# Larger first transfers, a new order of loads and weights, and exponentials kept in PSUM, in a fused gated-attention and feed-forward kernel

## The chip, the cores and the metric

The kernel runs on one core of a Trainium2 chip. The core has five engines that run side by side and meet only at semaphores: TensorE (PE, matrix products; PEld is its loading of weights), VectorE (DVE), ScalarE (ACT), GpSimd (POOL) and SyncE (SP, which here issues transfers). Transfers between main memory and the on-chip memory SBUF are carried by 16 DMA engines. PE writes its results to PSUM, a second on-chip memory of eight banks[...].

The metric is the device time of one execution in microseconds (us), as a median over runs. All line numbers are those of the kernel before.

## What is computed

Two stages, one behind the other. The first is a recurrence over time with a forget gate per channel; the second is a feed-forward layer on its result, with a gate through a ReLU.

```python
# q, k, v, f_logit: 4 batches x 8 heads x 768 steps x 48 channels
f = 1.0 / (1.0 + np.exp(-f_logit))
state = zeros((B, H, D, D))
for t in range(S):
    state = f[:, :, t, :, None] * state + einsum('bhd,bhe->bhde', k[:, :, t], v[:, :, t])
    y[:, :, t] = einsum('bhd,bhde->bhe', q[:, :, t], state)

x = y.transpose(0, 2, 1, 3).reshape(3072, 384)
gate = maximum(x @ w_gate, 0.0)          # 384 x 1536
val = x @ w_val                          # 384 x 1536
out = gate * val @ w_out                 # 1536 x 384
```

Inputs and output are float32; the products run in bfloat16.

## The kernel before

**Steps.** Time is cut into six steps of 128 (`c` from 0 to 5). A step covers 128 positions of all four batches, 512 tokens. Inside a step the recurrence becomes matrix products. With `bneg = ln(1 + exp(-f_logit))`, the negative logarithm of the gate, PE forms running sums over the 128 positions (`cum`), ACT takes `exp(-sum)` for q and `exp(+sum)` for k, and the products of q and k with these go into the tile `hats`. The hats are transposed into `qkT`; PE forms scores from them, DVE masks the scores into `ptm`, PE forms `y` from `ptm`, from `vpad` (a padded bfloat16 copy of v, made by POOL) and from the state of the step before. ACT copies `y` to `xT`, the input of the feed-forward part. There PE multiplies with `wg` (gate), ACT takes the ReLU, PE multiplies with `wv` (value), DVE multiplies both into `gT` (all near L784 to L807), PE multiplies with `wo` (L819), ACT copies the result out of PSUM (L829) and SP stores it (L833).

**Step 0 is built in another way than the rest** (`fours = (0,)`, `attention_four`, L485). Its f, k and q come in with four successive positions of one head in one piece of 768 bytes, so that partition 4t+b holds positions 4t to 4t+3 of batch b. The loader `load_four` (L375) issues four transfers per tensor, one per batch. The step is worked in two halves of the heads, `hh`, and in each half in two pairs of positions, `z`. For each (hh, z) ACT makes the exponentials for q (L532, written to `expo` in SBUF) and those for k (L535, in place in PSUM); the product with q is done by POOL for z=0 and by DVE for z=1 (L538), the one with k by DVE (L543). L555 transposes, L564 (DVE) and L563 (ACT) copy to `qkT`, L574 forms scores, L581 masks, L733 forms `y`, L750 makes `xT`.

**Loads of later steps** (`load`, L393) bring one tensor for two batches each ("f1.0" is f of step 1, batches 0 and 1), in pieces of 192 bytes, issued by SP. **Weights** come in nine blocks (`wg0` to `wo2`), issued by POOL (`load_w`, L409), converted to bfloat16 on the way. The order of the first transfers is written by hand:

```python
first = ("f0 k0 q0 v0.0 v0.1 wg0~8.0 wv0~8.5 wg1~14.5 wv1~15.3 wg2~17.5 wv2~18.3 f1.0@wv1 k1.0 q1.0 v1.0 "
         "wo0~23 wo1~25.5 f1.1@wo0 k1.1 wo2~28 q1.1 v1.1").split()
```

A number after `~` is the earliest time at which the planner may place the issue; `@wv1` makes SP wait until wv1 has landed. Loads from step 2 on wait for the third load before them (`flight = 3`) and for their buffer.

**The order on each engine** comes from a planner (`Plan.schedule`, L90). Every operation is entered with what it reads and writes, a price (`occ`, `lat`), a priority and the PSUM banks that it opens; banks are lent from groups with limits (L294). The planner always takes the operation that can start earliest by its own clock, then the one of lower priority number, and so writes one fixed order per engine. Landing times of transfers are estimates too: a queue in which each transfer takes `flow` us. On the chip each engine follows its order strictly and stops at the semaphore of the first operation that isn't ready. The waits are derived from the plan (`needs`, L171).

**Fillers.** Where the plan leaves PE idle before 17 us, products with a tile of zeros (L880) are put in, so many as fit in the planned gap:

```python
gap, each = op.start - at, 0.44 if at < 4.5 else 0.23
if begun and op.start <= warm_until:
    for _ in range(int((gap - 0.05) / each)):
        busy.append((op, warm))
```

Of the kernel before, what the change touches and what calls it, by code (L numbers as in the profile page):

```python
# [5 lines left out]
AF = mybir.ActivationFunctionType  # L6
# [5 lines left out]
class Op:  # L12
# [1 line left out]

    __slots__ = ("eng", "emit", "reads", "writes", "occ", "lat", "prio", "opens", "deps",
                 "idx", "start", "end", "pos", "inc", "sem", "val", "snap", "n_left", "users", "ready",
                 "after", "follows", "flow", "goal", "floor")

    def __init__(self, eng, emit, reads, writes, occ, lat, prio, opens=(), after=(), follows=()):
        self.eng, self.emit, self.reads, self.writes = eng, emit, reads, writes  # L20
        self.occ, self.lat, self.prio, self.opens = occ, lat, prio, list(opens)
        self.after, self.follows = list(after), list(follows)
        self.users = []
        self.inc = False
        self.sem = None
        self.val = 0
        self.start = None
        self.flow = None
        self.floor = 0.0


class Bank:
# [9 lines left out]
class Plan:  # L42
# [47 lines left out]
    def schedule(self, banks):  # L90
        self.link()
        for op in self.ops:
            op.n_left = len(op.deps)
            op.ready = op.floor
            for d in op.deps:
                d.users.append(op)
        free = dict(self.free0)
        waiting = {e: [] for e in self.ENGINES}
        order = {e: [] for e in self.ENGINES}
        for op in self.ops:  # L100
            if op.n_left == 0:
                waiting[op.eng].append(op)
        slots = [{"ap": ap, "tile": None, "at": at} for ap, at in banks]
        used = {}
        left = len(self.ops)
        flow_free = 0.0

        def banks_for(op):
            n, group = len(op.opens), op.opens[0].group
            if used.get(group, 0) + n > self.limits[group]:  # L110
                return None
            idle = [s for s in slots if s["tile"] is None or all(o.start is not None for o in s["tile"].ops)]
            idle.sort(key=lambda s: s["at"])
            return idle[:n] if len(idle) >= n else None

        while left:
            pick = None
            for e in self.ENGINES:
                for op in waiting[e]:
                    at = max(free[e], op.ready)  # L120
                    slot = ()
                    if op.opens:
                        slot = banks_for(op)
                        if slot is None:
                            continue
                        at = max(at, slot[-1]["at"])
                    key = (at, op.prio, op.idx)
                    if pick is None or key < pick[0]:
                        pick = (key, op, slot)
            if pick is None:  # L130
                raise RuntimeError("no op can be scheduled: " + repr(
                    [(e, len(waiting[e])) for e in self.ENGINES]))
            (at, _, _), op, slot = pick
            e = op.eng
            waiting[e].remove(op)
            for tile, s in zip(op.opens, slot):
                if s["tile"] is not None:
                    for o in s["tile"].ops:
                        op.deps[o] = "war"
                s["tile"] = tile  # L140
                tile.ap, tile.slot = s["ap"], s
                used[tile.group] = used.get(tile.group, 0) + 1
            op.start, op.end = at, at + op.occ + op.lat
            if op.flow is not None:
# [24 lines left out]
        return order  # L169
# [47 lines left out]
def bass_hgrn2_outer__then__ffn_reglu_kernel(  # L217
# [12 lines left out]
    x_way = {0: "tiled", 1: "tiled", 2: "tiled", 3: "xbar", 4: "xbar", 5: "xbar"}  # L230
    flight = 3
    wsteps = 3
    first = ("f0 k0 q0 v0.0 v0.1 wg0~8.0 wv0~8.5 wg1~14.5 wv1~15.3 wg2~17.5 wv2~18.3 f1.0@wv1 k1.0 q1.0 v1.0 "
             "wo0~23 wo1~25.5 f1.1@wo0 k1.1 wo2~28 q1.1 v1.1").split()
    B, H, S, D = q.shape
    C = 128
    NC = S // C
# [53 lines left out]
    zeros = sb("zeros", [128, 512], BF16)  # L291
    banks = [nc.alloc_psum_tensor(f"ps{i}", [128, 512], F32) for i in range(8)]

    pl = Plan({"bc": 2, "bc4": 4, "tp": 2, "tp4": 4, "s": 4, "y": 2, "kv": 1, "f": 4})  # L294
    add = pl.add
    gp, ve, sc, te, sy = nc.gpsimd, nc.vector, nc.scalar, nc.tensor, nc.sync
    engine = {"POOL": gp, "DVE": ve, "ACT": sc}
# [77 lines left out]
    def load_four(n, c):  # L375
        t = ld[n]
        row = NL[n] * 2 * HD

        def go():
            ops = []  # L380
            for b in range(B):
                src = bass.AP(tensor=srcs[n].tensor, offset=b * H * S * D + c * C * D,
                              ap=[[4 * D, 32], [S * D, H], [1, 4 * D]])
                dst = bass.AP(tensor=t, offset=b * row + slot_of(n, c, 0) * 2 * HD, ap=[[4 * row, 32], [4 * D, H], [1, 4 * D]])
                ops.append(sy.dma_start(dst, src))  # L385
            return ops
        last = tails.get("load")
        op = add("SP", go, [], in_keys(n, c, 0, B), occ=1.5, lat=0.9, prio=c * 100, follows=[last] if last else [])
        tails["load"] = op
        dma(op, f"{n}{slot_of(n, c, 0)}", 2.4, 4)  # L390
        return op

    def load(n, c, b0, b1, after=()):  # L393
# [3 lines left out]
                      ap=[[D, C], [S * D, (b1 - b0) * H], [1, D]])  # L397
        dst = t[:, slot_of(n, c, b0 // 2), :, :, :].rearrange("p b h d -> p (b h) d")
        op = add("SP", lambda: sy.dma_start(dst, src), [], in_keys(n, c, b0, b1),
                 occ=0.8 * (b1 - b0), lat=0.9, prio=c * 100, after=after,  # L400
                 follows=[last] if last else [])
        tails["load"] = op
        dma(op, f"{n}{slot_of(n, c, b0 // 2)}", 1.0 * (b1 - b0))
        return op

    WJ = NJ // wsteps
# [2 lines left out]
    def load_w(nm, s, at):  # L409
# [4 lines left out]
        else:  # L414
# [1 line left out]
                          ap=[[DFF, 128], [128 * DFF, NK], [1, WJ * 128]])  # L416
            dst = (wg if nm == "wg" else wv)[:, :, s * WJ * 128:(s + 1) * WJ * 128]
        last = tails.get("load_w")
        op = add("POOL", lambda: gp.dma_start(dst, src), [], [f"{nm}{s}"], occ=0.8, lat=1.2, prio=0,
                 follows=[last] if last else [])  # L420
        op.floor = at
        tails["load_w"] = op
# [3 lines left out]
    loads, done = [], {}  # L426
    for item in first:
        item, _, at = item.partition("~")
        item, _, behind = item.partition("@")
        need = [done[behind]] if behind else []  # L430
        if item[0] == "w":
            op = load_w(item[:2], int(item[2:]), float(at))
        elif "." in item:
            c, pr = (int(x) for x in item[1:].split("."))
            op = load(item[0], c, 2 * pr, 2 * pr + 2, need)
        else:
            op = load_four(item[0], int(item[1:]))
        done[item] = op
        if item[0] != "w":
            loads.append(op)  # L440
# [44 lines left out]
    def attention_four(c):  # L485
# [17 lines left out]
        for hh in range(2):  # L503
# [23 lines left out]
            for z in range(2):  # L527
# [1 line left out]
                ex = expo[:, e0 + i0:e0 + i0 + 2, 0, hh * HD // 2:(hh + 1) * HD // 2]  # L529
                hi = (h0 + i0) % NH  # L530
                his = (hi, hi + 1)
                add("ACT", lambda ex=ex, b_=bc[z]: sc.activation(  # L532
                    ex, b_.ap[:, 0:HD].rearrange("p (i e) -> p i e", i=2), AF.Exp, scale=-1.0), [bc[z]],
                    [f"expq{e0 + i0}_{hh}"], prio=R + z, **act_t(HD))
                add("ACT", lambda b_=bc[z]: sc.activation(b_.ap[:, 0:HD], b_.ap[:, 0:HD], AF.Exp, scale=1.0), [bc[z]],  # L535
                    [bc[z]], prio=R + z, **act_t(HD))
                e = "DVE" if z else "POOL"
                add(e, lambda e=e, ex=ex, hi=hi, hs=hs, i0=i0: engine[e].tensor_tensor(  # L538
                    hats[:, hi:hi + 2, 0, hs, 0:D], by_i["q"][:, i0:i0 + 2, hs, :],
                    ex.rearrange("p i (h d) -> p i h d", h=4), ALU.mult),  # L540
                    key["q"] + [f"expq{e0 + i0}_{hh}"] + [f"hats{x}" for x in his], [f"hq{x}_{hh}" for x in his], prio=R + z + 1,
                    **elem_t(e, HD))
                add("DVE", lambda b_=bc[z], hi=hi, hs=hs, i0=i0: ve.tensor_tensor(  # L543
                    hats[:, hi:hi + 2, 1, hs, 0:D], by_i["k"][:, i0:i0 + 2, hs, :],
# [338 lines left out]
    for op in order["PE"]:  # L883
        gap, each = op.start - at, 0.44 if at < 4.5 else 0.23
        if begun and op.start <= warm_until:
            for _ in range(int((gap - 0.05) / each)):
                busy.append((op, warm))
        begun = True
        at = op.start + op.occ
# [81 lines left out]
```

## Time and profile before

| | |
|---|---|
| median of 13 runs | 209.63 us |
| lowest and highest | 207.66 and 211.77 us |
| the profiled execution | 211.5 us |
| its span, first to last instruction | 209.8 us |
| PE busy | 190.9 us (91%) |
| DVE, ACT, POOL busy | 104.9, 110.4, 79.5 us |
| read from main memory, written to it | 25.95 MB, 4.72 MB |
| mean granted clock of PE | 0.967 of full |

The profile is of one execution. Its time stands 1.9 us above the median, and 1.7 us of it lie around the span. Busy time of PE is not PE at its peak: products with a lower clock, and the 9.1 us of fillers (24 of L880), count as busy.

The issues of transfers, with the median time from issue to landing, are these (KB is the size in SBUF; a weight block is read at twice that):

```profile
v_in<-in_v_dram SPq DMA_DIRECT2D x12, 384.0 KB, 5.3
out_dram<-osb SPq DMA_DIRECT2D x24, 192.0 KB, 2.2
...
wg<-in_moe_w_gate_dram POOLq DMA_DIRECT2D x3, 384.0 KB, 6.6
wv<-in_moe_w_val_dram POOLq DMA_DIRECT2D x3, 384.0 KB, 7.7
wo<-in_moe_w_out_dram POOLq DMA_DIRECT2D x3, 384.0 KB, 12.7
...
f_in<-in_f_logit_dram SPq DMA_DIRECT2D x4, 192.0 KB, 3.0
k_in<-in_k_dram SPq DMA_DIRECT2D x4, 192.0 KB, 3.4
q_in<-in_q_dram SPq DMA_DIRECT2D x4, 192.0 KB, 4.6
```

"SPq" is SP's work of issuing, not the transfer itself. The last three rows are the four pieces each of step 0.

### The profile page before, as it was taken

To read this page: it belongs to the slowest core of one execution; us is meant where nothing else is said; L and a number is where in the kernel's file an instruction comes from. 1 tells how busy PE (TensorE), PEld (TensorE's weight loads), DVE (VectorE), ACT (ScalarE), POOL (GpSimd) and SP (SyncE) were. 2 spreads that over 40 slices of the span, in tenths; PEclk is the share of its full clock that TensorE was granted. 3 is DMA by queue.
4 is the path that set the end of the run, shared out by engine and by line. 5 is a ranking of instruction groups with operands and counts; after the bars stand their busy time and mean duration, and the time that the engine had idled before them with its cause. 6 is when DMAs were issued, how large, how long until landed. Compare 5 with 4: busy or idle time off the path is not lost.

```text
span 209.8 us, 4328 instructions
## 1 busy us (share of the span) xinstructions
PE 190.9 (91%) x1724; PEld 109.7 (52%) x1743; DVE 104.9 (50%) x183; ACT 110.4 (53%) x239; POOL 79.5 (38%) x112
## 2 busy tenths in 40 slices
PE   7824779999999799999999998996999999999994
PEld 2413458645677585455555554553546554445562
DVE  7008377643817969657277353734545333323210
ACT  2840224583488688867738755564434334443411
POOL 8805920026196885966643643323410000000000
PEclk9995858999999999999999999999999999999999
DMA  4999799999589999999899996997962111111112
GB/s 142 260 176 171 106 199 188 193 230 220 138 188 240 197 220 176 183 199 214 177 205 140 194 205 123 219 177 144 194 139 60 54 38 41 38 38 38 38 49 105
DMA packets 115076, 31.74 MB, mean 151 GB/s; under 512 B 105072, under 2 KB 115056, under 8 KB 115056
## 3 DMA queue, kind: packets, MB, share of 16 engines
q1 hardware_dynamic: 111072, 27.93, 65.5%
q0 software_dynamic: 3984, 3.54, 11.0%
q8 instruction: 14, 0.23, 0.5%
q14 instruction: 6, 0.05, 0.2%
HBM read 25.95 MB, written 4.72 MB: 146 GB/s over the span
## 4 chain that ended last, share of the span: by engine, by line
PE 81%; DMA 7%; SPq 4%; ACT 3%; DVE 2%; issue 2%; DVEq 0%
PE ps L796 43%; PE ps L819 21%; DMA q_in<-in_q_dram 4%; SPq L385 3%; PE ps L706 3%; DMA qkT<-hats 3%; PE ps L733 2%; PE ps L767 2%; PE ps L676 2%; PE ps L640 1%; PE ps L555 1%; PE ps L880 1%; PE ps L743 1%; PE ps L739 1%; PE ps L574 1%
## 5 line engine op out<-in xcount | busy, mean ns | idle before, releaser
L806 DVE TENSOR_TENSOR gT<-relu,ps 128x512 bf16<-128x512 bf16 (+1 forms) x82 | 50.5, 620 | 58.5 <-PE ps L796 44.5
L802 ACT ACTIVATE relu<-ps 128x512 bf16<-128x512 f32 (+1 forms) x82 | 44.5, 545 | 31.7 <-PE ps L796 29.2
L796 PE MATMUL ps<-xT,wv 128*128 128x512 bf16 (+1 forms) x243 | 60.2, 355 | 0.3 <-issue 0.2
L796 PE MATMUL ps<-xT,wg 128*128 128x512 bf16 (+1 forms) x231 | 57.6, 355 | 1.4 <-ACT xT L750 0.6
L819 PE MATMUL ps<-wo,gT 128*128 128x384 bf16 x288 | 52.1, 326 | 0.0
L819 PEld LDWEIGHTS ps<-wo,gT 128*128 128x128 bf16 x288 | 27.0, 98 | 19.1
L796 PEld LDWEIGHTS ps<-xT,wg 128*128 128x128 bf16 x246 | 23.1, 99 | 20.0 <-ACT xT L750 0.9
L796 PEld LDWEIGHTS ps<-xT,wv 128*128 128x128 bf16 x246 | 22.9, 98 | 19.9
L662 POOL TENSOR_TENSOR hats<-k_in,expo 128x384 bf16<-128x384 f32 x20 | 19.9, 997 | 35.6 <-ACT expo L650 35.4
L711 DVE TENSOR_TENSOR ptm<-ps,tri 128x512 bf16<-128x512 f32 x40 | 26.0, 685 | 10.4 <-PE ps L706 10.4
L829 ACT ACTIVATE osb<-ps 128x384 f32<-128x384 f32 x24 | 11.7, 488 | 31.5 <-PE ps L819 31.4
L665 POOL TENSOR_TENSOR hats<-q_in,expo 128x384 bf16<-128x384 f32 x20 | 19.8, 997 | 10.6 <-DMA q_in<-in_q_dram 10.6
L482 POOL TENSOR_TENSOR st<-ssum,dec 128x384 bf16<-128x384 f32 x16 | 13.3, 829 | 16.2 <-DVE ssum L480 16.2
L697 POOL CAST vpad<-v_in 128x384 bf16<-128x384 f32 x24 | 11.6, 504 | 3.7 <-DMA v_in<-in_v_dram 3.7
L650 ACT ACTIVATE expo<-ps 128x384 f32<-128x384 f32 x20 | 9.8, 491 | 2.4 <-PE ps L643 2.2
L480 DVE TENSOR_TENSOR ssum<-ps,st 128x384 f32<-128x384 f32 x16 | 8.9, 554 | 4.3 <-PE ps L767 4.2
L706 PE MATMUL ps<-qkT 48*128 48x128 bf16 x160 | 7.9, 219 | 2.9 <-DMA qkT<-hats 2.6
L631 ACT ACTIVATE f_in<-f_in 128x768 f32<-128x768 f32 x10 | 8.4, 841 | 3.0 <-DMA f_in<-in_f_logit_dram 2.9
L652 ACT ACTIVATE expo<-ps 128x384 f32<-128x384 f32 x20 | 9.9, 496 | 0.0
L750 ACT ACTIVATE xT<-ps 128x384 bf16<-128x384 f32 x12 | 5.8, 491 | 6.9 <-PE ps L733 6.9
L706 PEld LDWEIGHTS ps<-qkT 48*128 48x128 bf16 x160 | 4.5, 94 | 8.9 <-DMA qkT<-hats 4.1
L880 PE MATMUL ps<-zeros 128*128 128x512 bf16 x24 | 9.1, 528 | 0.1
(81 smaller groups left out, 158.8 us busy)
## 6 DMA issues: line engine op xcount, KB each, us to landing
v_in<-in_v_dram SPq DMA_DIRECT2D x12, 384.0 KB, 5.3
out_dram<-osb SPq DMA_DIRECT2D x24, 192.0 KB, 2.2
f_in<-in_f_logit_dram SPq DMA_DIRECT2D x10, 384.0 KB, 5.1
k_in<-in_k_dram SPq DMA_DIRECT2D x10, 384.0 KB, 5.5
q_in<-in_q_dram SPq DMA_DIRECT2D x10, 384.0 KB, 5.8
wg<-in_moe_w_gate_dram POOLq DMA_DIRECT2D x3, 384.0 KB, 6.6
wv<-in_moe_w_val_dram POOLq DMA_DIRECT2D x3, 384.0 KB, 7.7
wo<-in_moe_w_out_dram POOLq DMA_DIRECT2D x3, 384.0 KB, 12.7
```

What stands on the lines that cost most here:

```text
L482: add("POOL", lambda: gp.tensor_tensor(t4(s_new), t4(tmp), rate, ALU.mult), [key] + dk, [f"S{b}_{c % 2}"], prio=P + 8, **pool_t(HD))
L662: add("POOL", lambda: gp.tensor_tensor(hk, kin[:, b % 2, :, :], ex[:, 1, :].rearrange("p (h d) -> p h d", h=H), ALU.mult), in_keys("k", c, ...
L665: add("POOL", lambda: gp.tensor_tensor(hq, qin[:, b % 2, :, :], ex[:, 0, :].rearrange("p (h d) -> p h d", h=H), ALU.mult), in_keys("q", c, ...
L697: add("POOL", lambda: gp.tensor_copy(vout, vin.rearrange("p (n j) d -> p n j d", j=2)), in_keys("v", c, b, b + 1) + [f"vpad{vi}"], [f"v_{v ...
L706: mm = te.matmul(s.ap[:, p * C:(p + 1) * C], tokens(c, b, 1, p, lo, lo + D), tokens(c, b, 0, p, lo, lo + D))
L711: add("DVE", lambda j=j, s=s: ve.tensor_tensor(ptm[mi][:, j, :, :], s.ap[:, :].rearrange("p (n t) -> p n t", n=NP), mask, ALU.mult), [s, " ...
L796: mm = te.matmul(bank.ap[:, 0:n], wt[:, kt, j * 128:(j + 1) * 128], xT[xi][:, kt, n0:n1], start=(kt == 0), stop=(kt == NK - 1))
L802: add("ACT", lambda: sc.activation(relu[ri][:, 0:n], gate.ap[:, 0:n], AF.Relu), [gate], [f"relu{ri}"], prio=P, **act_t(n))
L806: add("DVE", lambda: ve.tensor_tensor(gT[gi][:, j, n0:n1], relu[ri][:, 0:n], val.ap[:, 0:n], ALU.mult), [val, f"relu{ri}"], [f"gT{gi}_{j}_ ...
L819: mm = te.matmul(o[b].ap[:, 0:DM], gT[gi][:, j, b * C:(b + 1) * C], wo[:, j, :], start=(j == 0), stop=(j == NJ - 1))
L829: add("ACT", lambda b=b, oi=oi: sc.activation(osb[oi][:, :], o[b].ap[:, 0:DM], AF.Copy), [o[b]], [f"osb{oi}"], prio=P, **act_t(DM))
L880: return te.matmul(spare[:, 0:WARM], zeros[:, 0:128], zeros[:, 0:WARM], start=True, stop=True, skip_group_check=True)
```

## The change

Five things are done.

1. `load_four` issues one transfer per tensor in place of four, with the same layout in SBUF: the 128 partitions and 8 pieces of 768 bytes each are given as one access pattern.
2. The hand-written order: all weights stand behind the loads of v of step 0, and the loads of step 1 have no `@` waits.
3. Each item of that order has a landing time behind `=`, which the planner takes in place of its own estimate (new field `land`). `~` still gives the earliest issue. Weight issues get priority 50 in place of 0, and the prices of transfers are lower.
4. In step 0, for z=1, ACT writes the exponentials of q to a PSUM bank of the group `bc4` in place of `expo`, and DVE's product reads them there. The limit of the group goes from 4 to 6. POOL's product (z=0) still reads SBUF.
5. Fillers fill 0.7 of a gap in place of the gap less 0.05 us.

```diff
+            if op.land is not None:
+                op.end = max(op.end, op.land)
+                flow_free = max(flow_free, op.end - 0.8)
+            elif op.flow is not None:
...
-    first = ("f0 k0 q0 v0.0 v0.1 wg0~8.0 wv0~8.5 wg1~14.5 wv1~15.3 wg2~17.5 wv2~18.3 f1.0@wv1 k1.0 q1.0 v1.0 "
-             "wo0~23 wo1~25.5 f1.1@wo0 k1.1 wo2~28 q1.1 v1.1").split()
+    first = ("f0=5.2 k0=7.4 q0=9.6 v0.0=11.4 v0.1=13.0 wg0=15.4~11.3 wv0=17.4~11.3 wg1=19.4~14 wv1=21.4~14 wg2=23.4~17 "
+             "wv2=25.4~17 wo0=28~20 wo1=30.5~22 wo2=33~24 f1.0=24 k1.0=33 q1.0=35 v1.0=37 f1.1=38.6 k1.1=40.2 q1.1=42 "
+             "v1.1=43.6").split()
...
-    pl = Plan({"bc": 2, "bc4": 4, "tp": 2, "tp4": 4, "s": 4, "y": 2, "kv": 1, "f": 4})
+    pl = Plan({"bc": 2, "bc4": 6, "tp": 2, "tp4": 4, "s": 4, "y": 2, "kv": 1, "f": 4})
...
-        def go():
-            ops = []
-            for b in range(B):
-                src = bass.AP(tensor=srcs[n].tensor, offset=b * H * S * D + c * C * D,
-                              ap=[[4 * D, 32], [S * D, H], [1, 4 * D]])
-                dst = bass.AP(tensor=t, offset=b * row + slot_of(n, c, 0) * 2 * HD, ap=[[4 * row, 32], [4 * D, H], [1, 4 * D]])
-                ops.append(sy.dma_start(dst, src))
-            return ops
+        src = bass.AP(tensor=srcs[n].tensor, offset=c * C * D, ap=[[4 * D, 32], [S * D, B * H], [1, 4 * D]])
+        dst = bass.AP(tensor=t, offset=slot_of(n, c, 0) * 2 * HD, ap=[[row, 128], [4 * D, H], [1, 4 * D]])
...
-        dma(op, f"{n}{slot_of(n, c, 0)}", 2.4, 4)
+        dma(op, f"{n}{slot_of(n, c, 0)}", 2.3)
...
-                 occ=0.8 * (b1 - b0), lat=0.9, prio=c * 100, after=after,
+                 occ=0.5 * (b1 - b0), lat=0.9, prio=c * 100, after=after,
...
-        dma(op, f"{n}{slot_of(n, c, b0 // 2)}", 1.0 * (b1 - b0))
+        dma(op, f"{n}{slot_of(n, c, b0 // 2)}", 0.9 * (b1 - b0))
...
-        op = add("POOL", lambda: gp.dma_start(dst, src), [], [f"{nm}{s}"], occ=0.8, lat=1.2, prio=0,
+        op = add("POOL", lambda: gp.dma_start(dst, src), [], [f"{nm}{s}"], occ=0.8, lat=1.2, prio=50,
...
-                add("ACT", lambda ex=ex, b_=bc[z]: sc.activation(
-                    ex, b_.ap[:, 0:HD].rearrange("p (i e) -> p i e", i=2), AF.Exp, scale=-1.0), [bc[z]],
-                    [f"expq{e0 + i0}_{hh}"], prio=R + z, **act_t(HD))
+                eq = Bank("bc4") if z else None
+                eqk = eq if z else f"expq{e0 + i0}_{hh}"
+                add("ACT", lambda ex=ex, b_=bc[z], eq=eq: sc.activation(
+                    eq.ap[:, 0:HD].rearrange("p (i e) -> p i e", i=2) if eq else ex,
+                    b_.ap[:, 0:HD].rearrange("p (i e) -> p i e", i=2), AF.Exp, scale=-1.0), [bc[z]],
+                    [eqk], prio=R + z, opens=[eq] if z else [], **act_t(HD))
...
-                    ex.rearrange("p i (h d) -> p i h d", h=4), ALU.mult),
-                    key["q"] + [f"expq{e0 + i0}_{hh}"] + [f"hats{x}" for x in his], [f"hq{x}_{hh}" for x in his], prio=R + z + 1,
+                    eq.ap[:, 0:HD].rearrange("p (i h d) -> p i h d", i=2, h=4) if eq
+                    else ex.rearrange("p i (h d) -> p i h d", h=4), ALU.mult),
+                    key["q"] + [eqk] + [f"hats{x}" for x in his], [f"hq{x}_{hh}" for x in his], prio=R + z + 1,
...
-            for _ in range(int((gap - 0.05) / each)):
+            for _ in range(int(0.7 * gap / each)):
```

The orders that the planner writes from this differ as follows. SP issues f, k, q, both loads of v and then all eight loads of step 1 without a wait. POOL's order is: product with q (hh=0), wg0, cast of v (batch 0), product with q (hh=1), three more casts, wv0, wg1, wv1, wg2, wv2, wo0, wo1, wo2. PE has 1, 7, 1, 2 and 4 fillers at the places that had 2, 13, 1, 3 and 6. The running sums of step 1's first two batches stand among the 256-column products of step 0's feed-forward part; they stood among its 512-column products.

More of the change, by code (lines that the diff above doesn't have):

```diff
@@ L16 @@
                  "idx", "start", "end", "pos", "inc", "sem", "val", "snap", "n_left", "users", "ready",
-                 "after", "follows", "flow", "goal", "floor")
+                 "after", "follows", "flow", "goal", "floor", "land")
     def __init__(self, eng, emit, reads, writes, occ, lat, prio, opens=(), after=(), follows=()):
@@ L29, in __init__ @@
         self.floor = 0.0
+        self.land = None
 class Bank:
@@ L143, in schedule @@
             op.start, op.end = at, at + op.occ + op.lat
-            if op.flow is not None:
+            if op.land is not None:
+                op.end = max(op.end, op.land)
+                flow_free = max(flow_free, op.end - 0.8)
+            elif op.flow is not None:
                 begin = max(op.end, flow_free)
@@ L377, in load_four @@
         row = NL[n] * 2 * HD
-        def go():
-            ops = []
-            for b in range(B):
-                src = bass.AP(tensor=srcs[n].tensor, offset=b * H * S * D + c * C * D,
-                              ap=[[4 * D, 32], [S * D, H], [1, 4 * D]])
-                dst = bass.AP(tensor=t, offset=b * row + slot_of(n, c, 0) * 2 * HD, ap=[[4 * row, 32], [4 * D, H], [1, 4 * D]])
-                ops.append(sy.dma_start(dst, src))
-            return ops
+        src = bass.AP(tensor=srcs[n].tensor, offset=c * C * D, ap=[[4 * D, 32], [S * D, B * H], [1, 4 * D]])
+        dst = bass.AP(tensor=t, offset=slot_of(n, c, 0) * 2 * HD, ap=[[row, 128], [4 * D, H], [1, 4 * D]])
         last = tails.get("load")
-        op = add("SP", go, [], in_keys(n, c, 0, B), occ=1.5, lat=0.9, prio=c * 100, follows=[last] if last else [])
+        op = add("SP", lambda: sy.dma_start(dst, src), [], in_keys(n, c, 0, B), occ=0.7, lat=0.9, prio=c * 100, follows=[last] if last else [])
         tails["load"] = op
-        dma(op, f"{n}{slot_of(n, c, 0)}", 2.4, 4)
+        dma(op, f"{n}{slot_of(n, c, 0)}", 2.3)
         return op
@@ L428, in bass_hgrn2_outer__then__ffn_reglu_kernel @@
         item, _, at = item.partition("~")
-        item, _, behind = item.partition("@")
-        need = [done[behind]] if behind else []
+        item, _, land = item.partition("=")
         if item[0] == "w":
@@ L434, in bass_hgrn2_outer__then__ffn_reglu_kernel @@
             c, pr = (int(x) for x in item[1:].split("."))
-            op = load(item[0], c, 2 * pr, 2 * pr + 2, need)
+            op = load(item[0], c, 2 * pr, 2 * pr + 2)
         else:
             op = load_four(item[0], int(item[1:]))
+        op.land = float(land)
         done[item] = op
@@ L537, in attention_four @@
                 e = "DVE" if z else "POOL"
-                add(e, lambda e=e, ex=ex, hi=hi, hs=hs, i0=i0: engine[e].tensor_tensor(
+                add(e, lambda e=e, ex=ex, hi=hi, hs=hs, i0=i0, eq=eq: engine[e].tensor_tensor(
                     hats[:, hi:hi + 2, 0, hs, 0:D], by_i["q"][:, i0:i0 + 2, hs, :],
-                    ex.rearrange("p i (h d) -> p i h d", h=4), ALU.mult),
-                    key["q"] + [f"expq{e0 + i0}_{hh}"] + [f"hats{x}" for x in his], [f"hq{x}_{hh}" for x in his], prio=R + z + 1,
+                    eq.ap[:, 0:HD].rearrange("p (i h d) -> p i h d", i=2, h=4) if eq
+                    else ex.rearrange("p i (h d) -> p i h d", h=4), ALU.mult),
+                    key["q"] + [eqk] + [f"hats{x}" for x in his], [f"hq{x}_{hh}" for x in his], prio=R + z + 1,
                     **elem_t(e, HD))
```

## The prediction

> **What bounds the kernel now.** I read the page's slices first: they say where the matrix engine stands still.
>
> ```profile
> PE   7824779999999799999999998996999999999994
> ...
> PEclk9995858999999999999999999999999999999999
> DMA  4999799999589999999899996997962111111112
> ```
>
> A slice is 5.2 us. From the seventh slice on PE is 90% busy or more nearly everywhere; before that it is idle, or at half its clock. The same by stage (busy us and instructions of PE, PEld, DVE, ACT, POOL; then clock, DMA share, GB/s):
>
> ```profile
> 0.00:8.00 8.00, 6.10 (x18) 2.02 (x19) 3.71 (x13) 3.18 (x4) 7.36 (x22) 1.00 0.64 187
> 8.00:16.20 8.20, 3.91 (x39) 2.36 (x38) 0.02 (x1) 4.69 (x12) 1.65 (x3) 0.98 1.02 198
> 16.20:29.80 13.60, 8.61 (x103) 5.79 (x104) 9.31 (x16) 2.96 (x4) 9.43 (x13) 0.63 0.92 152
> 29.80:38.90 9.10, 9.05 (x113) 7.50 (x114) 6.38 (x17) 3.98 (x10) 0.00 (x0) 0.83 1.26 189
> 38.90:61.40 22.50, 22.45 (x212) 12.67 (x213) 10.65 (x18) 13.99 (x33) 9.29 (x12) 1.00 1.01 202
> 61.40:100.00 38.60, 37.17 (x525) 24.40 (x528) 29.24 (x53) 29.66 (x73) 28.27 (x36) 1.00 1.06 198
> 100.00:150.00 50.00, 46.95 (x399) 25.36 (x403) 25.80 (x40) 30.04 (x65) 20.74 (x26) 1.00 0.97 179
> ```
>
> After 29.8 us PE misses little (0.1 of 31.6 us up to 61.4, then 1.4 and 3.1). Its work from there is the same in both kernels, so the end moves with the start of the feed-forward part. What holds that start is in the chain of waits and the timeline (start, duration, engine, line):
>
> ```profile
> 8.18 7.91 DMA q_in<-in_q_dram
> ...
> 17.50 1.02 DVE hats L543 x2
> 18.52 0.05 issue
> 18.56 1.89 PE ps L555 x16
> 20.45 2.48 PE ps L880 x6
> ```
> ```profile
> 8.84 7.59 SPq L399 DMA_DIRECT2D v_in<-in_v_dram  x2
> ...
> 16.18 1.40 DVE L538 TENSOR_TENSOR hats<-q_in,expo 128x384 bf16<-128x384 f32 x1 [11.21 <-DMA q_in<-in_q_dram]
> ...
> 28.26 0.37 SPq L399 DMA_DIRECT2D f_in<-in_f_logit_dram  x1
> 28.67 5.43 SPq L399 DMA_DIRECT2D k_in<-in_k_dram  x1
> 34.14 6.86 SPq L399 DMA_DIRECT2D q_in<-in_q_dram  x1
> ```
>
> q lands at 16.1 although ACT has finished all exponentials at about 12.7. From there a serial chain of 13.66 us leads to the first feed-forward matmul at 29.76 (its first with wv at 30.37). That chain is the prize; the rest is bound by PE.
>
> **What the Trainium skill says.** "DMA: Bandwidth & Descriptors", section Queues, rings and completion order: the 16 DMA engines take turns, packet by packet, between the queues that have work. So weights (POOL's queue) and loads (SP's) divide the engines. The trace agrees and shows how unequally: between 28 and 41 us, with both queues full, five weight blocks landed (wg2 30.3, wv2 32.1, wo0 34.7, wo1 38.7, wo2 40.7), while f of step 1 took 13.0 us and k 14.0, against 3.7 us for an f load issued at 54.4. "SBUF — State Buffer", section Who interferes with whom: a VectorE instruction with two SBUF inputs and a GpSimd one that reads SBUF exclude each other for a whole instruction. It agrees: the L538 on DVE beside POOL's took 1399 ns, the second 545. "TensorE: Matmul & The Clock Gate", section What's actually happening: about 3.4 us idle halve the clock. It agrees: PE idles from 12.0 and the clock is 0.50 from 16 to 22.
>
> **The change part by part.** I follow the marks of before and move each.
>
> *Transfers of step 0.* Twelve issues of 0.61 to 0.76 us on SP become three; f's fourth issue ended at 3.54, q's at 8.8. The 2.36 MB are the same, in pieces of the same 768 B. In the window 2:4 the DMA share is 0.70, so data move from about 2.6; in 4:6 they moved at 277 GB/s. At that rate all three are in at 2.6 + 2360/277 = 11.1, landed at 11.7 with the 0.6 us that f took after its last byte (worked out at 5.4, landed 6.0). The other end is the skill's HBM limit per core, 358 GB/s (the same DMA page, Specifications): 2.6 + 6.6 + 0.6 = 9.8. Part of the 277 was the pacing of issues (196.6 KB per 0.65 us is 302 GB/s), so I take 10.7 for q and 5.7 for f. In before the pieces of q met wg0 and wv0, issued at 7.9 and 8.8: the traffic fell from 265 GB/s (8:10) to 141 (10:12). The change puts wg0 behind POOL's product with q, so this meeting goes. **Saved: 16.1 - 10.7 = 5.4 us.** Late next is ACT: its exponentials of the first half of the heads end at 10.9 now, at 10.6 with f at 5.7, just in time; were q at 9.8 only about 0.4 of that 0.9 would count.
>
> *q exponentials in PSUM.* DVE's L538 then has one SBUF input, as L543 has, which takes 0.54 beside a running POOL. 1.40 becomes 0.55. From q to the transposes: 0.55 + 1.02 + 0.05 in place of 2.4. **Saved: 0.8.** ACT writes 128x384 to PSUM as often as it wrote SBUF (0.43 each; its in-place ones took 0.44), so nothing there. Two more banks of the bc4 group are taken from banks idle at that time.
>
> *Clock and fillers.* PE ends its sums near 11.3 and starts transposes at 12.4 in place of 18.56: no 3.4 us of idling. The 16 transposes cost 1.0 (the second set at full clock: 1.07) in place of 1.89: **0.85**. The six fillers before the scores ended 1.36 us after ACT's copy (22.86 against 21.50); there are now four, 0.9 us at full clock, covered by that copy of 1.02: **1.35**. Elsewhere seven fillers in place of thirteen precede the sums and end before bneg is there; if the gap let the clock fall, the transposes would cost the 0.85 again.
>
> *POOL's queue.* Order now: product (hh0), wg0, cast of v (b0), product (hh1), three casts, wv0, wg1, wv1, wg2, wv2, wo x3. The second product stands behind a wait for v. v0.0 follows q: 0.39 MB at the 195 GB/s of 12:14 is 2.0 us, so it lands near 13.2; cast 0.5, product 1.0: 14.7. Its readers, the second transposes, start at about 15.4 (12.4 + 1.0 + 1.02 of copy + 1.0 of scores). Hidden, with 0.7 to spare.
>
> *Feed-forward start.* From the second transposes to the first feed-forward matmul: 29.76 - 23.90 = 5.86, left as it is. 15.4 + 5.86 = 21.2: 8.6 us earlier, which is 5.4 + 0.8 + 0.85 + 1.35 and 0.2 of shorter gaps.
>
> *wv0.* It is issued behind the casts of v0.1. v0.1 lands 2.0 us after v0.0, slowed a little by wg0: 15.5. Two casts: 16.5. A weight landed 5.1 us after issue in a quiet queue (wg1, 21.2), 7.7 to 8.7 among others (wv2, wg0). Now SP's queue is full of step 1 behind it: bounds 5.1 and 10.2 (wv0 itself in before). I take 6.5: 23.0. It is wanted at 21.2 + 0.6 = 21.8, and in PE's order the second pair of attention and the states stand behind it. **Given back: 1.2.** So 30.37 becomes 23.0: 7.4.
>
> *Later weights and step 1.* At 2.6 us each: wg1 25.6, wv1 28.2, wg2 30.8, wv2 33.4, wo2 41; wanted, with before's distances, from 31.5 (38.9 - 7.4), about 37 and about 45. Covered. f of step 1 goes out without the wait of 11.8 us on SP, right behind v, lands near 19 to 23, and ACT wants it at about 25.5 (before its relus, in order). The other loads get 70 to 80 GB/s while weights run (f and k of step 1 together, 0.79 MB, from 28.3 to 42.7, with part of q): v1.1 near 47 in place of 53.4. PE wants these from about 40 on. Moving ACT's 4 us of step-1 exponentials among the 256-column relus makes ACT nearly full for 9 us; I put 0.4 lost there and in the new order later, between 1.5 gained (before has 4.5 us of PE idle from 61 to 150) and 2 lost.
>
> SP is also moved past: its stores now stand behind six loads of step 2, each waiting for the third load before it, so the first store (53.98 now) goes out near 53 for a result that is ready near 50. Four osb buffers cover that; otherwise ACT's copies would stop some 3 us.
>
> *The planner's own numbers* (landing times, prices, priority 50, one more field) cost nothing by themselves; they act through the orders, which I took as the changed kernel has them.
>
> **Sum:** 7.4 - 0.4 = 7.0. The profiled execution took 211.5 with a span of 209.8, 1.9 over the median of the runs (209.63). It would become 204.5 and 202.8; the median **202.6**.
>
> **The rivals.**
> (a) *Weights late.* wv0 takes 10 us or more: 26.5 or later. For: SP's loads are no longer held. Against: five weights in 13 us beside loads. Gain 30.37 - 26.5 - 0.4 = 3.5: 206.1.
> (b) *One transfer is no faster.* q at 11.7 and v after it: 1 us less, 203.6. For: a DMA share of 0.96 in 4:6. It lies in my range.
> (c) *Given back in step 1 and later.* PE's order is fixed, so one late load or full ACT stops all behind it. For: DMA share near 1 up to 150 us, and the two waits of about 3 us for qkT transposes. Against: PE hardly waited for a load after 29.8. Gain about 1.5: 208.
> (d) *Slower.* If packets favoured the loads as they now favour the weights, a weight block would move at 70 GB/s, 5.6 us each: from 17.3 wo2 would land at 17.3 + 8 x 5.6 = 62. The first output sums read all of wo; they started at 49.7 and read wo2 near 52. The point is wo2 at 52 plus 1; at 62 the end is some 5 us late after other work fills a part: 214. Against: the landings above.
>
> **How the numbers follow.** Forecast, with (b) in it, 0.64; (a) 0.18; (c) 0.09; (d) 0.09. What a measurement can tell from no change is 0.5%, 1.05 us. Of (c) about half falls within it: faster 0.86, same 0.05, slower 0.09. Range: below, q at 9.8, wv0 at 5.1 us and 1.5 gained later give 199.6; above, most of (a): 206.2.
>
> **What would show it.** The first feed-forward matmul near 21, the first with wv near 23, waiting for DMA; q landed near 10.7; DVE's first L538 at 0.55; PE clock 1.0 at the first transposes; no PE waits of over 1 us for weights later. I am wrong if the first product with wv is not before 26, or if PE idles over 4 us more between 30 and 150.

## The result, and the profile after

The changed kernel took 212.62 us in the median of 11 runs (210.87 to 214.99); the kernel before took 209.74 us in 48 runs (206.02 to 212.04). The medians lie 2.9 us apart (1.4%); the ratio on record, which is not formed from these medians, is 1.017, with a 95% interval of 1.013 to 1.022. So the change made the kernel slower. The runs of the changed kernel fall into six of 210.9 to 212.6 us and five of 214.3 to 215.0, and the profile shows one of the lower six, whose median of 211.5 lies 1.8 us above the kernel before; what sets the others apart is not known. The forecast was 202.6, with a range of 199.6 to 206.2. The profiled execution of the changed kernel took 211.1 us, its span 209.4.

The slices of its page, 5.2 us each:

```profile
PE   7496899599999997989899999959999999999994
...
PEclk9799699969999999999999999999999999999999
DMA  5999999999999999999989998961121111111112
```

PE is now busy for 90% or more from the sixth slice on (the fifth has an 8); before it was from the seventh. So the start-up did become shorter. But there is a 5 in the eighth slice (36.6 to 41.9 us), with a low clock behind it, and a 7, two 8s and a 5 follow, where the profile before had a 7, an 8 and a 6. The same by stage (busy us and instructions of PE, PEld, DVE, ACT, POOL; then clock, DMA share, GB/s):

```profile
22.00:38.00 16.00, 15.92 (x158) 11.06 (x160) 10.18 (x23) 10.35 (x25) 3.94 (x5) 0.91 1.24 187
38.00:42.00 4.00, 1.68 (x24) 1.15 (x23) 3.10 (x6) 0.00 (x0) 0.95 (x2) 0.99 1.14 215
42.00:46.00 4.00, 4.00 (x36) 1.36 (x38) 1.66 (x3) 2.34 (x4) 0.83 (x1) 0.58 1.06 209
...
60.00:100.00 40.00, 37.09 (x485) 23.94 (x487) 27.31 (x50) 29.69 (x75) 27.59 (x36) 1.00 1.09 205
100.00:150.00 50.00, 45.73 (x365) 24.19 (x370) 24.13 (x37) 24.92 (x53) 16.80 (x21) 1.00 0.78 156
```

Line numbers of the changed kernel lie two or three above those of before in most of this section (the feed-forward products are L799, their wo products L822, the transposes of hats L679, the state products L770, the casts of v L700). The first feed-forward product starts at 22.03 (29.76 before), the first with wv at 22.64 (30.37) and it waits for nothing. That is a lead of 7.7 us. It is spent in three places: 2.3 us of standing still before 41.5, about 1.7 us by the clock of 0.58 from 42 to 46, and 7.2 us of idle time from 60 to 150 (2.9 and 4.3), where the kernel before had 2.1 us in a second profile (e4 below) and 4.5 in the first.

What PE was doing as it stopped is in its timeline (start, duration, line; in brackets the idle time and who ended it):

```profile
37.19 0.61 PE L679 MATMUL ps<-ident,hats 128*128 128x128 bf16 x8
...
38.83 0.40 PE L709 MATMUL ps<-qkT 48*128 48x128 bf16 x8
41.49 0.34 PE L770 MATMUL ps<-vpad,hats 128*128 128x96 bf16 x4 [2.26 <-POOL vpad L700]
41.88 1.02 PE L799 MATMUL ps<-xT,wg 128*128 128x512 bf16 x2
```

By 37.2 PE works on the transposes of step 1, and at 39.2 it comes to a state product of step 1. That needs POOL's cast of v, which needs the load v1.0. Feed-forward products of step 0, whose weights and inputs are there, stand behind it and run at 41.88. The chain of waits shows the load that they all waited for, and later ones of the same kind:

```profile
17.89 22.98 DMA v_in<-in_v_dram
...
40.93 0.51 POOL vpad L700
41.49 0.34 PE ps L770 x4
41.88 2.30 PE ps L799 x5
...
86.81 6.64 DMA qkT<-hats
```

v1.0 was issued at 17.89 and took 23.0 us to land, beside the weights. On the page, the same chain by engine, and one group with the idle time before it, first of the changed kernel and then of the kernel before:

```profile
PE 44%; DMA 28%; SPq 10%; POOL 7%; issue 5%; ACT 4%; DVE 1%; POOLq 0%
...
L700 POOL CAST vpad<-v_in 128x384 bf16<-128x384 f32 x24 | 11.7, 504 | 20.5 <-DMA v_in<-in_v_dram 20.5
```
```profile
PE 81%; DMA 7%; SPq 4%; ACT 3%; DVE 2%; issue 2%; DVEq 0%
...
L697 POOL CAST vpad<-v_in 128x384 bf16<-128x384 f32 x24 | 11.6, 504 | 3.7 <-DMA v_in<-in_v_dram 3.7
```

PE was 81% of that chain before; now transfers, their issues and POOL hold 45% of it. POOL waited 20.5 us for v (3.7 before). POOL also makes the hats of the later steps, which stand behind these casts; so the hats come late, the transposes of them by DMA (`qkT<-hats`) come late, and PE waits: five times, 5.1 us in all between 60 and 150. In the longest of these waits, the 2.5 us before 138.69, it was not a cast but a load of q that POOL had waited for (2.0 us, to 130.1).

### The profile page after: what moved, and what is told of

Its sections match the earlier page's. It is cut to its first block, busy times and chain, and to the rows that moved or that the text cites. A ratio compares the mean times of both kernels' runs of the same rounds, so it can differ in the third digit from the quotient of the medians.

```text
span 209.4 us, 4312 instructions
## 1 busy us (share of the span) xinstructions
PE 189.4 (90%) x1714; PEld 107.9 (52%) x1733; DVE 104.2 (50%) x183; ACT 110.7 (53%) x239; POOL 79.2 (38%) x112
## 4 chain that ended last, share of the span: by engine, by line
PE 44%; DMA 28%; SPq 10%; POOL 7%; issue 5%; ACT 4%; DVE 1%; POOLq 0%
PE ps L799 26%; PE ps L822 15%; DMA v_in<-in_v_dram 13%; SPq L398 8%; DMA qkT<-hats 7%; DMA f_in<-in_f_logit_dram 5%; POOL hats L665 2%; DMA xT<-xn 2%; POOL st L481 2%; SPq L387 1%; POOL hats L668 1%; PE ps L709 1%; ACT relu L805 1%; POOL vpad L700 1%; PE ps L770 1%
## 5 line engine op out<-in xcount | busy, mean ns | idle before, releaser
L799 PE MATMUL ps<-xT,wv 128*128 128x512 bf16 (+1 forms) x243 | 60.7, 358 | 0.2
L799 PE MATMUL ps<-xT,wg 128*128 128x512 bf16 (+1 forms) x231 | 58.3, 359 | 1.7 <-ACT xT L753 0.8
L822 PE MATMUL ps<-wo,gT 128*128 128x384 bf16 x288 | 52.1, 326 | 0.0
L822 PEld LDWEIGHTS ps<-wo,gT 128*128 128x128 bf16 x288 | 27.2, 98 | 18.8
L799 PEld LDWEIGHTS ps<-xT,wv 128*128 128x128 bf16 x246 | 23.1, 99 | 20.9 <-issue 0.8
L799 PEld LDWEIGHTS ps<-xT,wg 128*128 128x128 bf16 x246 | 23.2, 99 | 19.8 <-ACT xT L753 0.9
L700 POOL CAST vpad<-v_in 128x384 bf16<-128x384 f32 x24 | 11.7, 504 | 20.5 <-DMA v_in<-in_v_dram 20.5
L759 ACT ACTIVATE xn<-ps 128x384 bf16<-128x384 f32 x12 | 5.9, 488 | 7.4 <-PE ps L746 4.6
L770 PE MATMUL ps<-vpad,hats 128*128 128x96 bf16 x80 | 6.8, 207 | 3.1 <-POOL vpad L700 2.9
```

Source lines behind the costliest of these rows:

```text
L700: add("POOL", lambda: gp.tensor_copy(vout, vin.rearrange("p (n j) d -> p n j d", j=2)), in_keys("v", c, b, b + 1) + [f"vpad{vi}"], [f"v_{v ...
L799: mm = te.matmul(bank.ap[:, 0:n], wt[:, kt, j * 128:(j + 1) * 128], xT[xi][:, kt, n0:n1], start=(kt == 0), stop=(kt == NK - 1))
L822: mm = te.matmul(o[b].ap[:, 0:DM], gT[gi][:, j, b * C:(b + 1) * C], wo[:, j, :], start=(j == 0), stop=(j == NJ - 1))
```

## The experiments

Theory A: the transfers of the change are good, and the loss is the new order of the engines. The planner wrote it from cheaper load prices and from landing times that are mostly earlier than the real ones, so the work of the next steps stands ahead of its data, and whole engines wait in front of it. A has two parts. A1 is the landing times written by hand (wv0 at 17.4 where it landed at 21.6, wo2 at 33 for 39.9, v1.0 at 37 for 40.9, v1.1 at 43.6 for 48.2; two were too late, f1.0 at 24 for 17.9 and k1.0 at 33 for 19.7). A2 is the prices of `load`, 1.0 and 1.8 us of issue and transfer for a load in place of 1.6 and 2.0, which also hold for steps 2 to 5. The rivals are that the transfers themselves do harm: step 1's loads and the weights starve one another, or the single transfers bring nothing.

### The changed transfers under the old order (e1)

The kernel before, with everything of the change except the planner's numbers. Orders are taken from the old plan; the weights are then moved behind v on POOL's queue, and the two waits of SP are dropped. The traces agree: but for the weights on POOL, the fillers, the twelve issues that became three and the bank of the exponentials, every engine does the same operations in the same sequence as in the kernel before.

```diff
-    pl = Plan({"bc": 2, "bc4": 4, "tp": 2, "tp4": 4, "s": 4, "y": 2, "kv": 1, "f": 4})
+    pl = Plan({"bc": 2, "bc4": 6, "tp": 2, "tp4": 4, "s": 4, "y": 2, "kv": 1, "f": 4})
...
+        go = lambda: sy.dma_start(dst, src)
...
+                eq = Bank("bc4") if z else None
...
+    done["wg0"].start = q0.start + 0.01
+    for i, n in enumerate(("wv0", "wg1", "wv1")):
+        done[n].start = c3.start + 0.01 * (i + 1)
+    order["POOL"].sort(key=lambda o: (o.start, o.pos))
...
+    for n in ("f1.0", "f1.1"):
+        for w in ("wv1", "wo0"):
+            done[n].deps.pop(done[w], None)
...
-            for _ in range(int((gap - 0.05) / each)):
+            for _ in range(int(0.7 * gap / each)):
```

> All of the change that the chip sees at the start (one transfer each for f, k, q, weights behind v, step 1 loaded without waits, q exponentials in PSUM, fewer fillers), but every engine keeps the order of the kernel before. Theory A, the loss is in the new order of the engines: the feed-forward part starts near 22 us, PE waits less than 1 us between 30 and 60, the end is 5 to 8 us earlier than before: 202 to 205 us. Theory B, the loss is in the transfers (step 1 starved behind the weights, whatever the order): PE stands still 2 us or more near 40 again, 209 to 212 us. Theory C, any lead is given back later because the DMA engines are full up to 150 us: no stall near 40, but 2 to 3 us more idle from 60 to 150 than before, 207 to 209 us.

Measured: 201.99 us, ratio to the kernel before 0.964 (0.960 to 0.969), at the fast end of what theory A expected. Its stages, and POOL's waits with their total, number and longest:

```profile
38.00:42.00 4.00, 3.95 (x23) 1.88 (x23) 1.84 (x4) 3.44 (x11) 3.12 (x4) 1.00 1.09 202
42.00:46.00 4.00, 4.00 (x31) 2.48 (x29) 1.23 (x3) 0.60 (x1) 1.67 (x3) 1.00 1.24 235
...
60.00:100.00 40.00, 38.52 (x484) 23.36 (x490) 28.11 (x50) 30.21 (x75) 30.30 (x39) 1.00 1.08 200
100.00:150.00 50.00, 49.53 (x410) 26.92 (x415) 27.09 (x43) 29.22 (x59) 17.74 (x23) 1.00 0.87 173
```
```profile
POOL hats L661 <- ACT expo L649: 36.5, 9, 16.8
...
POOL hats L664 <- DMA q_in<-in_q_dram: 3.1, 2, 1.6
```

The transfers are those of the changed kernel almost to the tenth: v1.0 landed at 41.2 (40.9), q1.0 at 35.3 (34.8), v1.1 at 48.4 (48.2), the last wo at 40.3 (39.9), and feed-forward began at 21.83 (22.03). Yet nothing stops at 40: PE still has feed-forward products of step 0 to do, and the first transposes of step 1 (L675) stand at 45.1, where they stood at 37.2 in the changed kernel. POOL waits for no load of v at all. So the change without the planner's numbers (the transfers, the exponentials in PSUM and the fillers together) gains 7.9 us against the 209.89 of the runs beside it, and the new orders cost 212.6 - 202.0 = 10.6 us in the medians, 9.4 in the spans of the two profiles. A is shown as far as the order goes; that the late loads do this harm whatever the order is refuted.

The sum on PE agrees. From 22 to 150 us PE idles 9.7 us in the changed kernel and 2.1 in this one; the cold stretch from 42 to 46 costs 1.7 more, and a colder one here (clock 0.85 against 0.91 from 22 to 38) gives 1.0 back. That is 8.3 of the 9.4 us between their spans (209.4 and 200.0).

### The changed order without the wo transfers (e2)

Here the three blocks of `wo` aren't loaded: GpSimd fills them with 0.01, and the products with wo run on that constant. It takes three of the nine weight transfers off the DMA engines and leaves the planner's input alone; v1.0 lands at 34.9 (40.9).

```diff
-        op = add("POOL", lambda: gp.dma_start(dst, src), [], [f"{nm}{s}"], occ=0.8, lat=1.2, prio=50,
+        op = add("POOL", (lambda: gp.memset(dst, 0.01)) if nm == "wo" else (lambda: gp.dma_start(dst, src)), [], [f"{nm}{s}"],
```

> The changed kernel with its order on every engine; the three transfers of wo are left out and the tile is filled with a constant by GpSimd (so the last products run on a constant). Theory B: v of step 1 lands some 6 us earlier, before 36 us, the wait for it at 39 to 41.5 and the cold clock behind it go, 4 us faster than the changed kernel: about 208.5 us. Theory A: the wait goes too, but the order of the later steps stays as it is, so it remains above the kernel before or near it: 208 to 210 us. Theory C: the gain is under 1.5 us: 211 us or more.

Measured: 207.45 us, 0.987 (0.982 to 0.992), a little faster than theory A (208 to 210) or B (208.5) expected. The stages:

```profile
38.00:42.00 4.00, 3.95 (x46) 2.36 (x45) 3.79 (x7) 2.77 (x4) 0.00 (x0) 1.00 1.20 221
...
60.00:100.00 40.00, 38.85 (x479) 24.49 (x483) 27.34 (x51) 31.04 (x80) 28.65 (x35) 1.00 1.09 200
100.00:150.00 50.00, 45.37 (x348) 23.43 (x351) 23.09 (x36) 23.05 (x45) 12.35 (x16) 0.97 0.70 139
```

With step 1's loads earlier, the stop at 40 is gone, and 5.2 us in all. The idle time from 60 to 100 falls too, from 2.9 to 1.2 us. Yet from 100 to 150 PE idles as long as in the changed kernel (4.6 us against 4.3). So the loss is two things: one at 40 us, where data of step 1 come late, and one in the later steps, of which the part behind 100 us doesn't hang on the traffic of the start.

### The single transfers alone (e3), and the kernel before again (e4)

e3 is the kernel before with one transfer each for f, k and q, everything else left, wg0 and wv0 in their old places included.

```diff
-            for b in range(B):
...
-                ops.append(sy.dma_start(dst, src))
...
+        go = lambda: sy.dma_start(dst, src)
...
-        dma(op, f"{n}{slot_of(n, c, 0)}", 2.4, 4)
+        dma(op, f"{n}{slot_of(n, c, 0)}", 2.4)
```

> The kernel before with one transfer each for f, k and q of step 0, nothing else, same order. If the number of issues sets when q lands: q lands 2 us or more earlier and the end is 2 us earlier, 207.7 us. If the weights in the same DMA engines set it: q within 1 us of 16.1, no change of over 0.5 us, 209.3 to 209.9 us.

> The kernel before once more, for a second profile. If the profile of before stands for its runs: feed-forward start within 0.5 us of 29.8 and a span of 207 to 210 us with 4 to 5 us of PE idle from 60 to 150. If that profile was an untypical one: start or idle differ by 1.5 us or more.

Measured: e3 203.70 us, 0.971 (0.967 to 0.975); e4, a single run, 209.26 us. In e3 q landed at 11.2 although wg0 and wv0 were issued at 7.9 and 8.8; feed-forward began at 22.67. SP's timeline and what PE waited for:

```profile
2.30 1.71 SPq L381 DMA_DIRECT2D q_in<-in_q_dram  x1
...
22.56 0.37 SPq L394 DMA_DIRECT2D f_in<-in_f_logit_dram  x1
```
```profile
PE ps L635 <- ACT bneg L628: 3.0, 1, 3.0
```

The one edit that replaces twelve issues by three gives 6.2 us by itself, three times the 2 us expected. It would give more, but f1.0, which waits on SP for wv1, is now late: issued at 22.56, landed at 38.0, and PE stands 3.0 us for the gate made from it. In e4 feed-forward begins at 29.89 (29.76 in the first profile of before), but the span is 207.5 (209.8) and PE idles 2.1 us from 60 to 150 (4.5). So the first profile, whose time stood above the median, had lost about 2 us in its second half, and e4 is the better measure there.

### Which numbers of the planner: landing times (e5), prices (e6), both (e7)

All three are the changed kernel with only the planner's numbers edited. e5 takes the measured landing times of the weights and of the loads from v1.0 to v1.1, e6 the old prices of `load`, e7 both.

```diff
-    first = ("f0=5.2 k0=7.4 q0=9.6 v0.0=11.4 v0.1=13.0 wg0=15.4~11.3 wv0=17.4~11.3 wg1=19.4~14 wv1=21.4~14 wg2=23.4~17 "
-             "wv2=25.4~17 wo0=28~20 wo1=30.5~22 wo2=33~24 f1.0=24 k1.0=33 q1.0=35 v1.0=37 f1.1=38.6 k1.1=40.2 q1.1=42 "
-             "v1.1=43.6").split()
+    first = ("f0=5.2 k0=7.4 q0=9.6 v0.0=11.4 v0.1=13.0 wg0=18.1~11.3 wv0=21.6~11.3 wg1=24.5~14 wv1=26.9~14 wg2=29.4~17 wv2=32.3~17 wo0=34.5~20 wo1=37.2~22 wo2=39.9~24 f1.0=24 k1.0=33 q1.0=35 v1.0=41 f1.1=42.8 k1.1=44.5 q1.1=46.6 v1.1=48.3").split()
...
-                 occ=0.5 * (b1 - b0), lat=0.9, prio=c * 100, after=after,
+                 occ=0.8 * (b1 - b0), lat=0.9, prio=c * 100, after=after,
...
-        dma(op, f"{n}{slot_of(n, c, b0 // 2)}", 0.9 * (b1 - b0))
+        dma(op, f"{n}{slot_of(n, c, b0 // 2)}", 1.0 * (b1 - b0))
```

> The changed kernel; only the landing times that the planner is told differ: those that were too early are set to what its own trace shows (wg0 18.1, wv0 21.6, wo2 39.9, v of step 1 at 41, then 42.8, 44.5, 46.6, 48.3), so every engine gets another order. Theory A1, the order is bad because these landing times are too early: no wait for v of step 1 at 40, GpSimd's waits for v fall from 20 us to under 5, 203 to 206 us. Theory A2, the order is bad because the loads of steps 2 to 5 are priced too low (which stays): the wait at 40 goes, those from 60 to 150 stay, 207 to 210 us. Theory A3, the orders differ by chance and neither input is the cause: anything from 205 to 214, with waits in other places.

> The changed kernel with the prices of the kernel before for the loads in pieces of 192 bytes (issue 0.8 and transfer 1.0 us per batch in place of 0.5 and 0.9), nothing else; landing times for step 1 are still those told. Theory A1: the wait at 40 stays, 210 to 213 us. Theory A2: the wait at 40 stays, but GpSimd's waits for v after 60 us fall to under 5 us, 207 to 209 us. Theory A3: as above, no pattern.

> Both at once: landing times as measured and the old load prices. Theory A1 or A2 or both together: 202 to 205 us, like the old order with the new transfers (202.0). Theory A3: 205 to 214.

The measured medians with their ratios to the kernel before (the runs of it beside e5 to e8 had a median of 210.46 us), and PE's idle time in three stretches of each profile (stretch less PE's busy time), beside those of the other kernels:

| kernel | median us | ratio (95%) | idle 22 to 60 | 60 to 100 | 100 to 150 |
|---|---|---|---|---|---|
| changed | 212.62 | 1.017 (1.013 to 1.022) | 2.5 | 2.9 | 4.3 |
| e5, landings as measured | 209.68 | 0.992 (0.989 to 0.995) | 0.6 | 3.5 | 3.8 |
| e6, old prices | 207.53 | 0.986 (0.982 to 0.990) | 1.5 | 2.5 | 1.8 |
| e7, both | 203.78 | 0.970 (0.966 to 0.974) | 0.6 | 0.0 | 3.6 |
| e8, see below | 202.83 | 0.965 (0.960 to 0.969) | 0.5 | 1.1 | 1.6 |
| e1, old order | 201.99 | 0.964 (0.960 to 0.969) | 0.1 | 1.5 | 0.5 |

e5 takes away the stop at 40 (PE works straight through from 38 to 44) and leaves the later idle time: the landing times act on step 1 alone and are worth 2.9 us, less than A1 expected of them alone (203 to 206 us). Its feed-forward part also begins 1.6 us later, at 23.66. e6 leaves a stop of 1.4 us between 38 and 42 and takes 2.9 us off the idle time behind 60: the prices act later, as A2 has it, and are worth 5.1 us (but POOL still waits 7.1 us for v behind 60, where under 5 was expected). Both together give 8.8 us, as expected. In e7 the stretch that was idle 2.9 us is full:

```profile
60.00:100.00 40.00, 40.00 (x501) 24.80 (x490) 28.67 (x52) 30.24 (x76) 27.48 (x35) 1.00 0.97 195
```

What is left from e7 to e1 is 1.8 us; e7 begins feed-forward at 23.45, e1 at 21.83. POOL's waits for the loads of later steps roughly go with PE's idle time behind 60: they are 3.1 us in e1, 8.4 in e4, 14 in e8 and in the first profile of before, 24 in e6 and e7, 30 in the changed kernel and 34 in e5. In e7 only 2.4 of the 24 us lie between 60 and 100, where PE never stops; 14.9 lie between 100 and 150, where it idles 3.6.

### The weights in their old place (e8)

e1 again, but POOL issues the weights where it did before.

```diff
-    done["wg0"].start = q0.start + 0.01
-    for i, n in enumerate(("wv0", "wg1", "wv1")):
-        done[n].start = c3.start + 0.01 * (i + 1)
-    order["POOL"].sort(key=lambda o: (o.start, o.pos))
```

> The old order of every engine with one transfer each, q exponentials in PSUM, fewer fillers and step 1 loaded without waits, but the weights issued where they were (wg0 and wv0 before the product with q). If placing the weights behind v matters: q or v later than in the old-order run, feed-forward start at 22.5 or later, 203 us or more. If it doesn't: q at 11.2 as in the run with one transfer alone, its 3.0 us wait for step 1's gate gone, 201 to 202 us.

Measured: 202.83 us, 0.965 (0.960 to 0.969), which can't be told from e1 and lies between the two expectations. q landed near 11.6, feed-forward began at 22.54 (21.83 in e1), and e3's 3.0 us for the gate of step 1 are gone; SP no longer waits for wv1. Putting the weights behind v matters by 0.7 us at the start and little in the end; the waits of SP for weights did matter once the start was shorter.

e1 is the fastest kernel of the study, 3.6% below the kernel before. Four runs that were planned have no measured time: the issue price without the transfer price (e9), the reverse (e10), the kernel before with nothing but the cheaper prices (e11), and a control that makes prices dearer (e12). So which of the two prices carries e6's effect is open. It is open too how much of it is the luck of one list of orders: four plans of the changed kernel were timed, and the effects of landings and prices roughly add up (2.9 + 5.1 against 8.8 by the medians; 5.3 + 6.6 against 10.0 by the ratios), which speaks against mere luck but doesn't exclude a part of it. That the new order costs the time is shown by e1; that it does so because the landing times and prices are too low is supported by e5 to e7, but not shown beyond chance.

## Why the prediction was wrong

**The start-up, by its own steps: right in the sum, with some luck.** q landed at 11.1 (10.7 forecast). DVE's first L538 (now L540) took 0.55 (0.55). The first 16 transposes took 1.05 at a clock of 1.0 (1.0). POOL's second product ended in time. Feed-forward began at 22.03 (21.2); wv0 landed at 21.6 (23.0), so there was no wait for it, and the first product with wv ran at 22.64: 7.7 us gained, 7.4 forecast. Two terms were off and cancelled: the feed-forward part could begin only 0.8 us later than forecast, and wv0 landed 1.4 us earlier. With seven fillers PE did go cold from 8 to 11 (clock 0.50), in the sums rather than in the transposes. And moving wg0 and wv0 behind q wasn't needed for q: e3 leaves them in place and has q at 11.2. In the kernel before the last of q's four pieces, issued just after wg0, took 7.9 us, the first two 3.4 and 3.5; a single transfer, issued at 2.3, is nearly through by then.

**The step that failed** is "Later weights and step 1", with its "Covered" and its 0.4 us lost, between 1.5 gained and 2 lost. In place of 0.4 the new orders lost 10.6 us in the medians, 9.4 in the profiles (e1 against the changed kernel). The landing times in it were good: v1.1 was put near 47 and landed at 48.2, wo2 near 41 and landed at 39.9; and the text says that PE wants step 1's loads "from about 40 on". What wasn't done is to put the two side by side for v1.0. It lands at 40.9, POOL casts it in 0.5, and in the new order the state product of step 1 that reads it stands ahead of feed-forward products that were ready.

**The premise behind it** was that PE's work "from there is the same in both kernels, so the end moves with the start of the feed-forward part". The work is the same, its order isn't. e1 has the shorter start and the old order, and takes 202.0, within 0.6 us of the forecast: the sum was in effect worked out for that kernel. The planner's own numbers were put at nothing because "they act through the orders", but the text follows those orders no further than the first loads of step 2; for all later steps it has only the 0.4 us. The prices that act there cost 5.1 us by themselves (e6).

**The rivals.** Rival (c), given back because PE's order is fixed and "one late load" stops all behind it, named the mechanism and priced it at 208. It came true at 40 us and again in the later steps, but it got 0.09, since PE had "hardly waited for a load" before. That evidence came from an order that the change threw away. The "two waits of about 3 us" that it counted for (c) were transfers on the chain (3.29 and 3.11 us); PE itself stood still for qkT there for 2.6 us in three waits, and in e4 for 0.2. Rival (d), the only one on the slower side, had a sign that was right and a cause that wasn't: wo2 landed at 39.9, not 62. Rivals (a) and (b) didn't occur. Of its own tests, "PE idles over 4 us more between 30 and 150" is the one that fired: 9.6 us in the changed kernel, 4.6 in the first profile of before.

## What to carry to other kernels

Where a planner writes the order, a change of its prices is a change of the whole program: list where each later operation moves, and put the real landing time of its data beside it, before costing anything at nothing. A landing time that is put too early can cost a stop of the engine with ready work behind it, as at 40 us here. To judge a bundle of edits, run the new transfers under the old order first, since here that separated a gain of 7.9 us from a loss of 10.6.

## What the runs showed of the hardware

- **Few large issues.** One transfer of 768 KB in SBUF landed 5.4 us after its issue (f), and q at 11.1 with f and k before it, at 359 GB/s from 4 to 6 us (the prediction's upper end was 358) and 327 from 6 to 8; the same data in twelve issues moved at 277 and less.
- **Unequal sharing.** A load of 384 KB took 20.5 us (q1.0) and 23.0 us (v1.0) beside weights that landed one every 2.2 to 3.5 us. "DMA: Bandwidth & Descriptors", section Queues, rings and completion order, of the Trainium skill says that queues with work take turns packet by packet. That is no equal share of bytes: from 23 to 40 us the weights moved 2.39 MB in the profile's 2823 packets, the loads 0.86 MB in 4511.
- **An issue can hold its engine.** The issue of f1.1 alone kept SP for 14.3 us (22.0 to 36.3), while q1.0 and v1.0 were still on their way; short ones took 0.4 to 0.7. What it waits for isn't shown.
- **The clock after a short stop.** PE stood still for 2.3 us (39.2 to 41.5) and ran at half clock from 42 to 45; 2.8 us before 8.0 were followed by half clock too. The skill's page "TensorE: Matmul & The Clock Gate", section What's actually happening, puts the limit at about 3.4 us; here less was enough. But 3.0 us in e3 (37.2 to 40.1) and 1.4 us in e6 were followed by full clock, so the length of a stop alone doesn't decide.
